# Attention and a gated feed-forward layer on one core: the gate's sigmoid computed as a tanh, single exps, and a new order of steps

## The chip, the core and the metric

The kernel runs on one core of one Trainium2 chip. The metric is the device time of one execution in microseconds (us); the number to be predicted is the median over several runs. The engines of the core have these names in the profile: PE is TensorE's matmul, PEld its weight load, DVE is VectorE, ACT is ScalarE, POOL is GpSimd, SP is SyncE, which here only issues DMAs.

## What is computed

Eight batches of 576 tokens. Attention is local: 8 heads of 64 channels, in blocks of 64 tokens. Its output x (4608 rows of 512 channels) goes through a feed-forward layer with a gate that is made by a short convolution along the tokens.

```python
scores = (1 / sqrt(64)) * q_c @ k_c.T          # blocks of 64 x 64
attn = exp(scores - max(scores)); attn = attn / (sum(attn) + 1e-9)
x = attn @ v_c                                  # heads side by side: 512 channels
h = maximum(x @ w_in, 0.0)                      # w_in 512 x 1024
conv_out[t] = sum over k of conv_w[k] * h[t + k - 1]
gate = 1.0 / (1.0 + exp(-conv_out))
out = (h * gate) @ w_out                        # w_out 1024 x 512
```

The three weight arrays come in 8-byte floats; q, k and v in 4-byte floats.

## The kernel before

**Precision.** Every operand of the two large products is split in a high and a low part (names ending in `_h` and `_l`), and a product is made as high times high, high times low and low times high.

**Attention.** The 4608 rows are 36 tiles of 128 (`att`, line 427). For the first 9 tiles q and k are loaded by rows (`load_rows`) and transposed on PE (`t_pe`, line 146) with an ACT copy behind it; for the others DVE transposes (`t_dve`, line 157). Then follow the scores on PE (line 173), `s_max` and `s_sub` on DVE (lines 183, 187), `s_exp` on ACT (line 192), `s_sum`, `s_eps`, `s_rec` on DVE (lines 196, 199, 202), `s_norm` on POOL (line 205), the transpose `p_pe` on PE (line 212) with `p_copy` on ACT, the product with v on PE (`attn_v`, line 225), and the split of the result by `x_hi` on ACT and `x_lo` on DVE (lines 249, 253).

**First product and gate.** The rows are also cut into 16 units of 288 tokens (`NU`, `HS`). For a unit and each of the 8 slices of 128 columns of `w_in`, `block` (line 477) issues 12 matmuls (`mm1`, line 262) into one of three PSUM buffers `h_ps`, `h_relu` and `c_mid` on ACT (lines 268, 273), `c_left` and `c_right` on DVE (lines 277, 283), `c_sig` on ACT (line 288), `c_mul` on DVE (line 291), which is the last reader of `h_ps` and frees it, `g_hi` on ACT (line 300) and `g_lo` on POOL (line 304).

**Second product.** For each of the 36 output tiles and each of the 8 slices, `mm2` (line 315) issues three matmuls into `o_ps`; after the eighth slice `o_copy` on ACT (line 320) moves the sum to SBUF and `o_store` on SP writes it out.

**Weights.** Ten slices of the two weight arrays (four of them half as wide) and the small conv_w are loaded and split in high and low by `split` (line 401): for one slice DVE does `w_mask`, `w_rest`, `w_low`, `w_sign`, `w_pow` (lines 344, 353, 357, 362, 370), ACT `w_bias`, `w_hi`, `w_lo_copy` (lines 349, 366, 381) and POOL `w_lo_big` (line 378). The raw bytes lie in one of two buffers until `w_sign` is done.

**The order.** The kernel collects all of this as steps (`step`, line 68), each with its engine, an assumed cost and a key. A planner (lines 584 to 677) goes through the steps with a model of engines and buffers: of the steps that can start within 0.6 us of the earliest on an engine it takes the one with the lowest key, with a penalty for a later start. The instructions are then issued in that order, and a chain of dependencies (lines 688 to 693) holds each engine to it. A key is the value written where the step is made, plus an offset by the kind of step (`by_step`), plus half an offset by chain (`by_chain`, line 566; a chain is the steps that share one `st`, in the order in which they were made). A step of ACT that needs another activation table costs the planner 1.28 us more (line 630). The `s_exp` steps of a unit wait for all `s_sub` steps of that unit, except in unit 0, so that they stand together:

```python
            if u == 0:
                group_ = []
            else:
                group_ = exps.setdefault(u, [])
```

Until the first `mm2`, the kernel puts transposes of a unit matrix into the gaps that the plan leaves on PE (line 685); they compute nothing that is used.

Of the kernel before, what the change touches and what calls it, by code (L numbers as in the profile page):

```python
# [23 lines left out]
AF = mybir.ActivationFunctionType  # L24
ALU = mybir.AluOpType
# [5 lines left out]
def attn_ffn(ctx: ExitStack, tc: tile.TileContext, q, k, v, w_in, conv_w, w_out, out):  # L31
    nc = tc.nc
# [9 lines left out]
    HS = S // 2  # L42
# [8 lines left out]
    scale = 1.0 / float(D) ** 0.5  # L51
# [13 lines left out]

    steps = []

    def step(eng, cost, key, fn, args=(), after=(), take=(), free=(), lag=0.0, table=None, port=False, bank=None):

        s = dict(eng=eng, cost=cost, key=key, fn=fn, args=args, after=[a for a in after if a], take=take, free=free,
                 lag=lag, table=table, port=port, bank=bank)
        steps.append(s)
        return s

# [208 lines left out]
            op0=ALU.mult, op1=ALU.add)  # L285

    def c_sig(st):
        nc.scalar.activation(out=st["c"], in_=st["c"], func=AF.Sigmoid)  # L288

    def c_mul(st):  # L290
        nc.vector.tensor_tensor(out=st["c"], in0=st["h"][:, st["i0"]:st["i0"] + HS], in1=st["c"], op=ALU.mult)  # L291

    def g_views(u, f):
        g0 = HS * u % GR
# [22 lines left out]

    def o_copy(st):
        st["os"] = work.tile([P, 2 * DM], F32, name="wt")[:, 0:DM]
        nc.scalar.copy(out=st["os"], in_=st["o"])  # L320

    def o_store(st, t):
        nc.sync.dma_start(out=out_rows[P * t:P * t + P, :], in_=st["os"])
# [100 lines left out]
            s8 = step("DVE", b, key + 0.04, w_lo, (st, lo), [s4, s7], free=["wv", "we"], port=True)  # L424
        return [s6, s8]

    def att(t, key, load_key, exps, writes):


        st = {}  # L430
        if t < NAT:
            r = "wslot" if t in W_ROWS else "slot"
            ld = step("SP", 1.25, load_key, load_rows, (st, t), take=[(r, st)], lag=3.3)
            tt = []
            for i in range(2):
                s = step("PE", 0.44, key - 3, t_pe, (st, i), [ld, before.get("t")], take=["h", "qk"[i] + "T"], free=[r] if i else [])
                before["t"] = s
                tt.append(step("ACT", 0.59, key - 3, t_copy, (st, i), [s], free=["h"]))
            slot_users.append(s)
        else:  # L440
            ld = group(t // TG)
            tt = [step("DVE", 0.7, key - 3, t_dve, (st, t, i), ld, take=["qk"[i] + "T"]) for i in range(2)]
            tt[1]["after"].append(tt[0])
            if t % TG == TG - 1:
                tt[1]["free"] = ["grp"]
        ldv = step("SP", 2.65, load_key + 0.05 if t < 5 else key - 8, load_v, (st, t), [before.get("v")], take=["v"], lag=1.66)
        tt[0]["after"] += [before["T"]] if t else []
        s = step("PE", 0.47, key, scores, (st,), tt + [before.get("s")], take=[("sx", st, "s")], free=["qT", "kT"], bank="sx")
        before.update(v=ldv, T=tt[1], s=s)
        s = step("DVE", 0.69, key, s_max, (st,), [s], take=["m"], bank="sx")  # L450
        s = step("DVE", 0.68, key, s_sub, (st,), [s], take=["e"], free=["m", ("sx", "s")], bank="sx")
        exps.append(s)
        s = step("ACT", 0.63, key + 8, s_exp, (st,), exps, table="exp")
        s["after"] = exps
        s = step("DVE", 0.68, key + 9, s_sum, (st,), [s], take=["z"])
        s = step("DVE", 0.17, key + 9, s_eps, (st,), [s], port=True)
        s = step("DVE", 0.2, key + 9, s_rec, (st,), [s])
        s = step("POOL", 1.05, key + 9, s_norm, (st,), [s], free=["z"], port=True)
        s = step("PE", 0.44, key + 12, p_pe, (st,), [s], take=["pt"], free=["e"])
        s = step("ACT", 0.59, key + 12, p_copy, (st,), [s], take=["pT"], free=["pt"])  # L460
        s = step("PE", 0.47, key + 14, attn_v, (st,), [s, ldv], take=[("sx", st, "x")], free=["pT", "v"], bank="sx")
        n = len(x_views(st, t, x_h)) - 1
        s = step("ACT", 0.58 + 0.15 * n, key + 14, x_hi, (st, t), [s] + writes, bank="sx")
        return step("DVE", 0.69 + 0.1 * n, key + 14, x_lo, (st, t), [s], free=[("sx", "x")], bank="sx")
# [12 lines left out]
    def block(key, u, f, after):  # L477
        st = {}
        s = step("PE", 1.6, key, mm1, (st, u, f), after, take=["h"])
        m = s  # L480
        s = step("ACT", 0.4, key + 2, h_relu, (st,), [s])
        s = step("ACT", 0.55, key + 2, c_mid, (st, u, f), [s, cw_done], take=["c"])
        s = step("DVE", 0.52, key + 2, c_left, (st, u, f), [s])
        s = step("DVE", 0.52, key + 2, c_right, (st, u, f), [s])
        s = step("ACT", 0.44, key + 2, c_sig, (st,), [s], table="sig")
        s = step("DVE", 0.45, key + 2, c_mul, (st,), [s], free=["h"])
        s = step("ACT", 0.44, key + 2.5, g_hi, (st, u, f), [s] + ring.get((u, f), []))
        s = step("POOL", 0.81, key + 2.5, g_lo, (st, u, f), [s], free=["c"], port=True)
        return m, s
# [10 lines left out]
    key_of = {}  # L500
# [5 lines left out]
    wi_done, wo_done, x_done, mm1_of, g_done, ring = {}, {}, {}, {}, {}, {}  # L506
# [15 lines left out]
    for n in range(FT // 2):  # L522
        wo(n, U[1] - 6 + 8.0 * n, 5.0 + 2 * n, lo_pool=LP[4 + n] == "1")

    exps = {}
    for u in range(NU + 1):

        for t in tiles_for[u] if u < NU else []:

            over = [v_ for v_ in range(NU) if any(HS * v_ - 2 < P * t + P and P * t < HS * v_ + HS + 2 for _ in (0,))]  # L530
            writes = [mm1_of[v_ - NX, f] for v_ in over if v_ >= NX for f in range(FT)]
            if u == 0:
                group_ = []
            else:
                group_ = exps.setdefault(u, [])
            x_done[t] = att(t, key_of[t], 0.1 + 0.5 * t if t < 5 else 4.5 + t, group_, writes)
        if u < NU:
            for f in range(FT):

# [5 lines left out]
        for i, t in enumerate(outs_in[u] if u <= NU - 1 else []):  # L545
            st = {}
            prev = None
            for f in range(FT):
                key = U[u + 1] + (U[u + 2] - U[u + 1]) * (i + f / FT) / len(outs_in[u]) + 0.3
                units = [v_ for v_ in range(NU) if HS * v_ < P * t + P and P * t < HS * v_ + HS]  # L550
                prev = step("PE", 0.7, key, mm2, (st, t, f), [prev] + wo_done[f] + [g_done[v_, f] for v_ in units],
                            take=["o"] if f == 0 else [])
                mm2_of[t, f] = prev
            s = step("ACT", 0.58, key + 1, o_copy, (st,), [prev], take=["wt"], free=["o"])
# [1 line left out]


    by_step = {
        "w_load": 7, "w_mask": -3.5, "w_bias": -4, "w_rest": -3, "w_low": -3.5, "w_pow": -13.5, "c_sum": -27.5, "c_pe":
        -4, "c_copy": -5.5, "w_hi": 14, "w_lo_big": -4.5, "w_lo_copy": 4, "load_rows": -0.5, "t_pe": -4, "t_copy": -7.5,  # L560
        "load_v": 6, "scores": -0.5, "s_max": 6, "s_sub": -7, "s_exp": -12.5, "s_sum": -4, "s_eps": -9, "s_rec": 4,
        "s_norm": -29.5, "p_pe": 4.5, "p_copy": 3.5, "attn_v": 3, "x_lo": 1, "mm1": -0.5, "h_relu": 1, "c_mid": 2,
        "c_left": 1.5, "c_right": 3.5, "c_sig": -4, "c_mul": 5.5, "g_hi": 2, "g_lo": 24, "o_copy": 1.5, "o_store": 9,
        "load_group": 15, "load_part": 1.5, "t_dve": 19
    }
    by_chain = [
# [9 lines left out]
    ]  # L576
    chains = {}
    for s in steps:
# [19 lines left out]
    free_at = dict.fromkeys(early, 0.0)  # L598
    free_at.update(SP=0.7, ACT=3.0)
    port, other, share = {"DVE": 0.0, "POOL": 0.0}, {"DVE": "POOL", "POOL": "DVE"}, {"DVE": 0.2, "POOL": 0.137}  # L600
    dma_free, table, kind, bank = 0.0, "exp", 0, {}
    left = [len(a) for a in befores]
    begin, end = [0.0] * n_, [0.0] * n_
    order_ = []
# [4 lines left out]
    while any(ready.values()):  # L609
        best = None  # L610
        for e, cand in ready.items():
            picks = []
            for i in cand:
                s = steps[i]
# [8 lines left out]
                else:  # L623
# [3 lines left out]
                    for o, until_ in bank.get(s["bank"], {}).items():  # L627
                        if o != e:
                            t = max(t, until_ + late[e])
                    if e == "ACT" and s["table"] not in (None, table):  # L630
                        t += 1.28
                    if e == "PE":
                        t += turn.get((kind, kinds.get(s["fn"], 0)), (0.0, 0.0))[0]
                        key -= 6.0 if kind == kinds.get(s["fn"], 0) == 1 else 0.0
# [6 lines left out]
        assert best, [(steps[i]["eng"], steps[i]["fn"].__name__, steps[i]["args"][1:]) for c in ready.values() for i in c]  # L641
        t, e, i = best
        s, cost = steps[i], steps[i]["cost"]
        if e == "ACT":
            table = s["table"] or table
        if e == "PE":
            cost += turn.get((kind, kinds.get(s["fn"], 0)), (0.0, 0.0))[1]
            kind = kinds.get(s["fn"], 0)
# [71 lines left out]
```

## Time and profile before

| | us |
|---|---|
| median of 3 runs (lowest to highest) | 526.4 (525.32 to 527.32) |
| the profiled execution, device time | 526.21 |
| its span in the trace | 524.4 |

The profile shows one execution. The span is the time between its first and its last recorded event; the device time of the same execution is 1.8 us longer. Matmuls are pipelined and their ends are modelled, so that the duration of one matmul row overlaps the next; where the text gives a price for a group of matmuls it is taken from the start of one group to the start of the next, as the chain of work that ended last gives it.

### The profile page before, as it was taken

To read this page: it belongs to the slowest core of one execution; us is meant where nothing else is said; L and a number is where in the kernel's file an instruction comes from. 1 tells how busy PE (TensorE), PEld (TensorE's weight loads), DVE (VectorE), ACT (ScalarE), POOL (GpSimd) and SP (SyncE) were. 2 spreads that over 40 slices of the span, in tenths; PEclk is the share of its full clock that TensorE was granted. 3 is DMA by queue.
4 is the path that set the end of the run, shared out by engine and by line. 5 is a ranking of instruction groups with operands and counts; after the bars stand their busy time and mean duration, and the time that the engine had idled before them with its cause. 6 is when DMAs were issued, how large, how long until landed. Compare 5 with 4: busy or idle time off the path is not lost.

```text
span 524.4 us, 13247 instructions
## 1 busy us (share of the span) xinstructions
PE 512.5 (98%) x5150; PEld 455.8 (87%) x5150; DVE 357.5 (68%) x732; ACT 363.7 (69%) x812; POOL 171.9 (33%) x237
## 2 busy tenths in 40 slices
PE   8889999999999999999999999999999999999997
PEld 8789886999888898989889898888989889989985
DVE  5889999657867478678677548675856876755320
ACT  4668889767775767687767657575686858686430
POOL 1424645442332333242412423232341414242220
PEclk9999999999999999999999999999999999999999
DMA  8899460353234534532355354233463121000101
GB/s 216 205 229 250 134 160 20 70 100 95 47 66 89 108 98 93 122 56 48 80 129 94 74 125 79 55 68 68 107 110 84 42 61 42 1 21 21 42 34 47
DMA packets 183170, 47.04 MB, mean 90 GB/s; under 512 B 175404, under 2 KB 175428, under 8 KB 183108
## 3 DMA queue, kind: packets, MB, share of 16 engines
q1 hardware_dynamic: 183108, 46.20, 39.8%
q8 instruction: 40, 0.66, 0.5%
q14 instruction: 22, 0.18, 0.1%
HBM read 36.72 MB, written 9.44 MB: 88 GB/s over the span
## 4 chain that ended last, share of the span: by engine, by line
PE 84%; DVE 8%; DMA 5%; ACT 1%; POOL 1%; issue 0%; SPq 0%; DVEq 0%; ACTq 0%
PE o_ps L315 37%; PE h_ps L262 37%; DMA qk<-in_moe_w_in 4%; PE sx_ps L225 3%; PE sx_ps L173 3%; PE pt_ps L212 3%; DVE wv L357 2%; DVE wt L344 1%; DMA qk<-in_moe_conv_w 1%; DVE wt L362 1%; DVE c L277 1%; DVE wv L353 1%; DVE c L283 1%; DVE c L291 1%; POOL wv L378 0%; PE h_ps L151 0%
## 5 line engine op out<-in xcount | busy, mean ns | idle before, releaser
L304 POOL TENSOR_TENSOR g_l<-c,g_h 128x288 fp32r<-128x288 f32 (+8 forms) x184 | 114.0, 635 | 231.1 <-ACT g_h L300 220.0
L315 PE MATMUL o_ps<-wo_h,g_h 128*128 128x512 f32 x288 | 118.1, 410 | 0.0
L315 PE MATMUL o_ps<-wo_l,g_h 128*128 128x512 f32 x288 | 113.4, 394 | 0.5 <-ACT wo_l L381 0.5
L315 PE MATMUL o_ps<-wo_h,g_l 128*128 128x512 f32 x288 | 113.5, 394 | 0.0
L277 DVE SCALAR_TENSOR_TENSOR c<-h_ps,cw,c 128x287 f32<-128x287 f32 (+1 forms) x128 | 65.4, 512 | 66.6 <-ACT c L273 66.1
L262 PE MATMUL h_ps<-x_h,wi_h 128*128 128x290 f32 x512 | 91.7, 301 | 1.8 <-DVE c L291 1.7
L262 PE MATMUL h_ps<-x_l,wi_h 128*128 128x290 f32 x512 | 90.1, 298 | 0.0
L262 PE MATMUL h_ps<-x_h,wi_l 128*128 128x290 f32 x512 | 89.8, 297 | 0.0
L262 PEld LDWEIGHTS h_ps<-x_h,wi_h 128*128 128x128 f32 x512 | 79.2, 189 | 10.6 <-DVE c L291 3.5
L268 ACT ACTIVATE h_ps<-h_ps 128x290 f32<-128x290 f32 x128 | 50.8, 397 | 37.3 <-PE h_ps L262 36.5
L300 ACT CAST g_h<-c 128x288 fp32r<-128x288 f32 (+8 forms) x184 | 59.6, 357 | 24.3 <-DVE c L291 16.6
L262 PEld LDWEIGHTS h_ps<-x_h,wi_l 128*128 128x128 f32 x512 | 76.3, 190 | 0.0
L262 PEld LDWEIGHTS h_ps<-x_l,wi_h 128*128 128x128 f32 x512 | 76.2, 189 | 0.0
L288 ACT ACTIVATE c<-c 128x288 f32<-128x288 f32 x128 | 55.7, 443 | 29.0 <-DVE c L283 28.1
L291 DVE TENSOR_TENSOR c<-h_ps,c 128x288 f32<-128x288 f32 x128 | 56.7, 450 | 27.4 <-ACT c L288 25.4
L273 ACT ACTIVATE c<-h_ps,cw 128x288 f32<-128x288 f32 x128 | 63.7, 499 | 7.2 <-POOL g_l L304 0.4
L283 DVE SCALAR_TENSOR_TENSOR c<-h_ps,cw,c 128x288 f32<-128x288 f32 (+1 forms) x128 | 65.6, 513 | 3.0
L315 PEld LDWEIGHTS o_ps<-wo_h,g_l 128*128 128x128 f32 x288 | 54.2, 188 | 12.4
L315 PEld LDWEIGHTS o_ps<-wo_h,g_h 128*128 128x128 f32 x288 | 54.3, 189 | 9.2 <-ACT wt L320 0.6
L315 PEld LDWEIGHTS o_ps<-wo_l,g_h 128*128 128x128 f32 x288 | 54.3, 188 | 8.0 <-ACT wo_l L381 0.8
L205 POOL TENSOR_TENSOR e<-e,z 128x512 f32<-128x512 f32 x36 | 38.1, 1072 | 64.8 <-DVE z L202 54.3
L320 ACT COPY wt<-o_ps 128x512 f32<-128x512 f32 x36 | 21.0, 585 | 24.5 <-PE o_ps L315 23.9
(50 smaller groups left out, 562.6 us busy)
## 6 DMA issues: line engine op xcount, KB each, us to landing
v<-in_v SPq DMA_DIRECT2D x144, 64.0 KB, 2.5
out<-wt SPq DMA_DIRECT2D x36, 256.0 KB, 2.1
qk<-in_q SPq DMA_DIRECT2D x96, 48.0 KB, 2.1
qk<-in_k SPq DMA_DIRECT2D x96, 48.0 KB, 2.2
qk<-in_moe_w_out SPq DMA_DIRECT2D x4, 1024.0 KB, 5.6
qk<-in_q SPq DMA_DIRECT2D x96, 24.0 KB, 1.9
qk<-in_k SPq DMA_DIRECT2D x96, 24.0 KB, 1.8
qk<-in_moe_w_in SPq DMA_DIRECT2D x4, 512.0 KB, 5.2
```

The costliest lines, as they stand in the source:

```text
L205: nc.gpsimd.tensor_tensor(out=st["e"], in0=st["e"], in1=st["z"].rearrange("p (h o) -> p h o", o=1).broadcast_to([P, H, C]), op=ALU.mult)
L262: nc.tensor.matmul(h_ps[:, 0:XU], lhsT=wt[:, f // 2, kt, P * (f % 2):P * (f % 2) + P], rhs=xt[:, u % NX, kt, :], start=n == 0, stop=n == 3 ...
L268: nc.scalar.activation(out=st["h"][:, 0:XU], in_=st["h"][:, 0:XU], func=AF.Relu)
L273: nc.scalar.mul(out=st["c"], in_=st["h"][:, i0:i0 + HS], mul=cw[:, FT + f:FT + f + 1])
L277: nc.vector.scalar_tensor_tensor(out=c[:, a:HS], in0=st["h"][:, i0 + a - 1:i0 + HS - 1], scalar=cw[:, f:f + 1], in1=c[:, a:HS], op0=ALU.mu ...
L283: nc.vector.scalar_tensor_tensor(out=c[:, 0:b], in0=st["h"][:, i0 + 1:i0 + 1 + b], scalar=cw[:, 2 * FT + f:2 * FT + f + 1], in1=c[:, 0:b], ...
L288: nc.scalar.activation(out=st["c"], in_=st["c"], func=AF.Sigmoid)
L291: nc.vector.tensor_tensor(out=st["c"], in0=st["h"][:, st["i0"]:st["i0"] + HS], in1=st["c"], op=ALU.mult)
L300: nc.scalar.copy(out=g_h[:, f, gs], in_=st["c"][:, cs])
L304: nc.gpsimd.tensor_tensor(out=g_l[:, f, gs], in0=st["c"][:, cs], in1=g_h[:, f, gs].bitcast(F32), op=ALU.subtract)
L315: nc.tensor.matmul(st["o"], lhsT=gt[:, f, o:o + P], rhs=wt[:, f, :], start=f == 0 and n == 0, stop=f == FT - 1 and n == 2)
L320: nc.scalar.copy(out=st["os"], in_=st["o"])
```

## The change

The sigmoid becomes a tanh of half the argument, `c_mul` becomes (1 + tanh) times h, and the factor 1/2 moves into `o_copy`. Each `s_exp` waits for its own `s_sub` alone. The planner loses its notion of activation tables, and takes 0.52 us for `c_mul` where it took 0.45. All offsets of the order are new. Of `by_chain` (221 numbers before, as many after) the first line is shown.

```diff
     def c_sig(st):
-        nc.scalar.activation(out=st["c"], in_=st["c"], func=AF.Sigmoid)
+
+        nc.scalar.activation(out=st["c"], in_=st["c"], func=AF.Tanh, scale=0.5)
 
     def c_mul(st):
-        nc.vector.tensor_tensor(out=st["c"], in0=st["h"][:, st["i0"]:st["i0"] + HS], in1=st["c"], op=ALU.mult)
+        nc.vector.scalar_tensor_tensor(
+            out=st["c"], in0=st["c"], scalar=1.0, in1=st["h"][:, st["i0"]:st["i0"] + HS], op0=ALU.add, op1=ALU.mult)
...
     def o_copy(st):
         st["os"] = work.tile([P, 2 * DM], F32, name="wt")[:, 0:DM]
-        nc.scalar.copy(out=st["os"], in_=st["o"])
+        nc.scalar.mul(out=st["os"], in_=st["o"], mul=0.5)
...
-        exps.append(s)
-        s = step("ACT", 0.63, key + 8, s_exp, (st,), exps, table="exp")
-        s["after"] = exps
+        s = step("ACT", 0.63, key + 8, s_exp, (st,), [s])
...
-        s = step("ACT", 0.44, key + 2, c_sig, (st,), [s], table="sig")
-        s = step("DVE", 0.45, key + 2, c_mul, (st,), [s], free=["h"])
+        s = step("ACT", 0.44, key + 2, c_sig, (st,), [s])
+        s = step("DVE", 0.52, key + 2, c_mul, (st,), [s], free=["h"])
...
     by_step = {
-        "w_load": 7, "w_mask": -3.5, "w_bias": -4, "w_rest": -3, "w_low": -3.5, "w_pow": -13.5, "c_sum": -27.5, "c_pe":
-        -4, "c_copy": -5.5, "w_hi": 14, "w_lo_big": -4.5, "w_lo_copy": 4, "load_rows": -0.5, "t_pe": -4, "t_copy": -7.5,
-        "load_v": 6, "scores": -0.5, "s_max": 6, "s_sub": -7, "s_exp": -12.5, "s_sum": -4, "s_eps": -9, "s_rec": 4,
-        "s_norm": -29.5, "p_pe": 4.5, "p_copy": 3.5, "attn_v": 3, "x_lo": 1, "mm1": -0.5, "h_relu": 1, "c_mid": 2,
-        "c_left": 1.5, "c_right": 3.5, "c_sig": -4, "c_mul": 5.5, "g_hi": 2, "g_lo": 24, "o_copy": 1.5, "o_store": 9,
-        "load_group": 15, "load_part": 1.5, "t_dve": 19
+        "w_load": 5, "w_mask": -5, "w_bias": -1.5, "w_rest": -2, "w_low": 1.5, "w_sign": 0.5, "w_pow": -2, "c_sum": -31,
+        "c_pe": 3, "c_copy": -5, "w_hi": -3.5, "w_lo_big": -3.5, "w_lo_copy": 2.5, "load_rows": 1, "t_pe": -8, "t_copy":
+        -7.5, "load_v": 7.5, "scores": -1, "s_max": 5.5, "s_sub": -9, "s_exp": -12.5, "s_sum": -4.5, "s_eps": -6,
+        "s_rec": 5.5, "s_norm": -23, "p_pe": 2.5, "p_copy": 1, "attn_v": 4, "x_hi": -3, "x_lo": 0.5, "mm1": -0.5,
+        "c_left": 3.5, "c_right": 3, "c_sig": 3.5, "c_mul": 5.5, "g_hi": 1.5, "g_lo": 36, "o_copy": -2.5, "o_store": 9,
+        "load_group": 10, "load_part": 2.5, "t_dve": 23
     }
     by_chain = [
-        -4, -51, -13, -46, -1, -24, -46, 4, 2, -2, 8, 9, -27, -24, -22, -1, 20, -9, 5, -4, 6, -9, -12, 38, 19, 3, 12,
...
+        8, -112, 1, -59, 11, 1, -56, 10, 23, 17, 25, 33, -10, -6, 0, 22, 6, 23, -6, -5, 23, -2, 15, 46, 6, 8, 17, 11, 7,
...
-                    if e == "ACT" and s["table"] not in (None, table):
-                        t += 1.28
```

## Rows read from the trace of the kernel before

**Rows 1.** The page: busy us of each engine (share of the span) xinstructions.

```profile
PE 512.5 (98%) x5150; PEld 455.8 (87%) x5150; DVE 357.5 (68%) x732; ACT 363.7 (69%) x812; POOL 171.9 (33%) x237
```

**Rows 2.** Three stretches: start:end length, busy us, granted clock, DMA share, GB/s.

```profile
0.00:38.40 38.40, 33.85 (x478) 31.09 (x479) 28.43 (x57) 22.20 (x38) 11.69 (x15) 1.00 0.88 217
38.40:90.00 51.60, 48.12 (x467) 42.77 (x466) 49.04 (x86) 46.13 (x88) 27.31 (x21) 1.00 0.59 145
90.00:520.70 430.70, 430.52 (x4210) 381.93 (x4209) 280.02 (x591) 294.82 (x687) 132.94 (x202) 1.00 0.34 71
```

**Rows 3.** Chain of work that ended last: start us, length us, engine, line, count.

```profile
99.10 1.09 PE sx_ps L173 x64
...
156.22 4.88 PE h_ps L262 x36
...
466.12 0.44 PE pt_ps L212 x4
...
481.25 8.26 PE o_ps L315 x36
```

**Rows 4.** PE's groups by line, 90 to 520.7 us: xcount | busy, mean ns | idle before.

```profile
L315 PE MATMUL o_ps<-wo_h,g_h 128*128 128x512 f32 x277 | 113.4, 409 | 0.0
...
L262 PE MATMUL h_ps<-x_h,wi_l 128*128 128x290 f32 x455 | 79.8, 297 | 0.0
...
L225 PE MATMUL sx_ps<-pT,v 64*64 64x64 f32 x960 | 19.4, 222 | 0.1
```

**Rows 5.** The same view from 38.4 to 90 us.

```profile
L262 PE MATMUL h_ps<-x_h,wi_h 128*128 128x290 f32 x60 | 11.3, 310 | 1.8 <-DVE c L291 1.7
...
L685 PE MATMUL o_ps<-ident 128*128 128x128 f32 x63 | 8.3, 274 | 0.0
L315 PE MATMUL o_ps<-wo_h,g_h 128*128 128x512 f32 x11 | 4.7, 430 | 0.0
```

**Rows 6.** Whom PE waited for, 38.4 to 90 us: us in total, times, longest.

```profile
PE h_ps L262 <- DVE c L291: 1.7, 3, 0.9
...
PE pt_ps L212 <- POOL e L205: 0.3, 1, 0.3
```

**Rows 7.** Table loads of ACT, whole run, by line: xcount | busy, mean ns | idle.

```profile
L288 ACT ACT_TABLE_LOAD x15 | 19.2, 1283 | 0.3
...
L192 ACT ACT_TABLE_LOAD x14 | 18.0, 1283 | 0.2
```

**Rows 8.** ACT in order of time: the table loads before 90 us.

```profile
44.70 1.28 ACT L288 ACT_TABLE_LOAD   x1
...
79.11 1.28 ACT L192 ACT_TABLE_LOAD   x1
...
86.22 1.28 ACT L288 ACT_TABLE_LOAD   x1
```

**Rows 9.** One stretch, with the columns of rows 2.

```profile
41.00:94.00 53.00, 49.45 (x501) 43.58 (x500) 51.44 (x91) 47.48 (x94) 29.10 (x21) 1.00 0.53 136
```

**Rows 10.** DVE's w_low: its 1024-wide form in the mean, and one.

```profile
L357 DVE SCALAR_TENSOR_TENSOR wv<-qk,wv 128x1024 f32<-128x1024 uint32 x6 | 8.7, 1458 | 0.0
...
42.77 1.22 DVE L357 SCALAR_TENSOR_TENSOR wv<-qk,wv 128x1024 f32<-128x1024 uint32 x1
```

**Rows 11.** DVE, by form: two-operand products and three-operand ones.

```profile
L291 DVE TENSOR_TENSOR c<-h_ps,c 128x288 f32<-128x288 f32 x128 | 56.7, 450 | 27.4 <-ACT c L288 25.4
...
L277 DVE SCALAR_TENSOR_TENSOR c<-h_ps,cw,c 128x288 f32<-128x288 f32 x64 | 32.9, 515 | 40.5 <-ACT c L273 40.3
...
L375 DVE SCALAR_TENSOR_TENSOR we<-wv,we 24x128 f32<-24x128 f32 x1 | 0.3, 280 | 0.0
...
L384 DVE TENSOR_TENSOR wt<-wt,we 24x128 f32<-24x128 f32 x1 | 0.3, 278 | 0.0
```

**Rows 12.** ACT, by form: a copy and a product with a constant.

```profile
L320 ACT COPY wt<-o_ps 128x512 f32<-128x512 f32 x36 | 21.0, 585 | 24.5 <-PE o_ps L315 23.9
...
L381 ACT ACTIVATE wi_l<-wv 128x512 fp32r<-128x512 f32 x4 | 2.5, 630 | 2.6 <-POOL wv L378 2.6
```

More of the change, by code (lines that the diff above doesn't have):

```diff
@@ L66, in attn_ffn, with step @@
     steps = []
-    def step(eng, cost, key, fn, args=(), after=(), take=(), free=(), lag=0.0, table=None, port=False, bank=None):
+    def step(eng, cost, key, fn, args=(), after=(), take=(), free=(), lag=0.0, port=False, bank=None):
         s = dict(eng=eng, cost=cost, key=key, fn=fn, args=args, after=[a for a in after if a], take=take, free=free,
-                 lag=lag, table=table, port=port, bank=bank)
+                 lag=lag, port=port, bank=bank)
         steps.append(s)
@@ L425, in split, with att @@
         return [s6, s8]
-    def att(t, key, load_key, exps, writes):
+    def att(t, key, load_key, writes):
         st = {}
@@ L523, in attn_ffn @@
         wo(n, U[1] - 6 + 8.0 * n, 5.0 + 2 * n, lo_pool=LP[4 + n] == "1")
-    exps = {}
     for u in range(NU + 1):
@@ L531, in attn_ffn @@
             writes = [mm1_of[v_ - NX, f] for v_ in over if v_ >= NX for f in range(FT)]
[L532 to L536, printed above, removed]
+            x_done[t] = att(t, key_of[t], 0.1 + 0.5 * t if t < 5 else 4.5 + t, writes)
         if u < NU:
@@ L600, in attn_ffn @@
     port, other, share = {"DVE": 0.0, "POOL": 0.0}, {"DVE": "POOL", "POOL": "DVE"}, {"DVE": 0.2, "POOL": 0.137}
-    dma_free, table, kind, bank = 0.0, "exp", 0, {}
+    dma_free, kind, bank = 0.0, 0, {}
     left = [len(a) for a in befores]
@@ L643, in attn_ffn @@
         s, cost = steps[i], steps[i]["cost"]
-        if e == "ACT":
-            table = s["table"] or table
         if e == "PE":
```

16 rows, old and new, of the table by_chain are left out of this document.

## The prediction

> **What bounds the kernel.** I began with the page's busy times [rows 1]: PE stands at 98% of the span, ACT at 69%, DVE at 68%. That PE is busy does not say that it does useful work: until the first `mm2` it also runs transposes that fill gaps. So the second view was the windows, cut where the trace changes: at 38.4 us, where the first `mm1` starts, and at 90 us, behind the last wait of PE for another engine that is more than a change from one kind of matmul to the next [rows 2]. The granted clock is 1.00 in all three, so every price of PE below is one of the 2.4 GHz level.
>
> Third, the chain of work that ended last, for prices from start to start [rows 3]: 36 matmuls of `mm1` take 4.88 us, so a group of 12 costs 1.627; 36 of `mm2` take 8.26, so three cost 0.688; two tiles of scores (or of `attn_v`) take 1.09, one 0.545; one `p_pe` 0.44. With the counts behind 90 us [rows 4], `mm1` is 455 x 3 / 12 = 113.75 groups, 185.1 us; `mm2` 277 groups, 190.6 us; attention 960 / 32 = 30 tiles at 2 x 0.545 + 0.44 = 1.53, 45.9 us. Together 421.6 of 430.7 us. What is left, 9.1 us or 2%, is the price of changing between kinds of matmul. **From 90 us on the kernel is PE's bare work**; nothing that ACT, DVE or POOL save there can show in the time, except as fewer changes of kind.
>
> Between 38.4 and 90 us it is otherwise. Useful are 15 groups of `mm1` (24.4 us), 11 of `mm2` (7.6) and a few tiles of attention; fillers take 8.3 us and PE waits 1.7 us for `c_mul` and 0.3 for `s_norm` [rows 5, 6]. What binds PE there is DVE: from 41 to 94 us it is busy 51.44 of 53.0 us, ACT 47.48 [rows 9]. DVE splits the weights and does the convolution of the first blocks at once. Ahead of 38.4 us DVE is busy 28.43 us and the DMA engines 88% [rows 2]: it is the loads that rule.
>
> **The change part by part.** The sum is made against the profiled execution, 526.21 us (span 524.4 and 1.8 around it); the median is 526.4, 0.2 above it.
>
> *Table loads.* 15 + 14 = 29 loads of 1.283 us go, 37.2 us of ACT [rows 7]. Behind 90 us lie 26 of them, 33.4 us, hidden by PE's own work; if that cover were gone (PE waiting for ACT), up to 33.4 us would show. Ahead of 90 us are three: at 44.70 and 86.22, each in front of a `c_sig`, whose `c_mul` frees the `h_ps` that an `mm1` wants, and at 79.11 in front of two exps [rows 8]. They cost at most 3 x 1.283 = 3.8 us, and nothing if DVE, full as it is, takes up what ACT gives. The nearest rows are PE's own waits for what hangs on these loads, 1.7 + 0.3 = 2.0 us [rows 6]; I take **-2.0**, ends 0 and -3.8.
>
> Between a load and the activation behind it the trace shows next to no idle time, 0.3 us over 15 loads [rows 7]. The Trainium skill ("ScalarE: Activation LUTs", section "What ACT_TABLE_LOAD costs") puts a drain of 1380 ns beside the load and 2.66 us on a switch; by that page three switches would be 8.0 us and this term, scaled alike, -4.2, for a time of 519.8. The trace does not agree, so the sum keeps 1.283.
>
> *tanh for sigmoid* is the same kind of activation on the same 128x288 tile; the scale of 0.5 is a constant of the instruction. I take 0; ACT has 51.6 - 46.13 = 5.5 us free in the middle stretch [rows 2], so that a few per cent on 15 of them would be covered.
>
> *`c_mul`* gets a third operand, a constant. With a constant such an instruction took 280 ns where a product of two took 278, at 24x128; `c_left`, whose scalar is a column of a tile, takes 515 where `c_mul` takes 450 [rows 11]. So a call costs 2 to 65 ns more; 15 calls lie ahead of the point where PE is full, 0.03 to 1.0 us. A gain is excluded, since the tiles stay and an operation is added. The constant is the nearer row: **+0.1**. The other 113 calls are up to 7.3 us of DVE, hidden since DVE is busy 280 of 430.7 us behind 90 [rows 2].
>
> *`o_copy`* as a product: a copy of 128x512 takes 585 ns, a product with a constant from SBUF 630 [rows 12]. All but the last are beside PE's work; the last is on the path, 0 to +0.05. I take 0.
>
> *Exps that no longer wait* for each other can start some us sooner in each unit. Behind 90 us PE stands 0.1 us for `attn_v` [rows 4] and has `mm1` and `mm2` queued, so nothing is gained; in a unit without such cover it would be one wait of `p_pe`, 0.3 us where it shows now [rows 6]. Counted in the term above.
>
> *The new order* moves every step on every queue. For SP I worked the keys of the loads out of the offsets: before and after, the first are one half slice of w_in, one full slice, then the rows of tiles 0 to 2, then two half slices (which change places), conv_w, the last half slice, the fourth slice; w_out follows. So the loads that rule the first 38.4 us come in nearly the same order, and I leave that stretch as it is. POOL has 51.6 - 27.31 = 24 us free in the middle stretch, and the DMA engines are at 59% there [rows 2]; so what is moved past their queues (`s_norm`, `g_lo`, `w_lo_big`, loads and stores) has room. A gain is bounded by all that PE now loses: 8.3 + 1.7 + 0.3 = 10.3 us in the middle, the 38.4 - 28.43 = 10.0 us in which DVE stands idle ahead of it, and 9.1 us of changes of kind, 29.4 together. The end below is in the rivals, +6.1. What a new order can do in the stretch that DVE binds is nearer to two rows: DVE's idle time there, 53.0 - 51.44 = 1.56 us [rows 9], and the passes that other engines stretch, such as `w_low`, 1458 ns in the mean where one alone took 1220, six times 0.24 = 1.4 us [rows 10]. That is 3.0 us; I take **-2.5**.
>
> *Sum:* -2.0 + 0 + 0.1 + 0 - 2.5 = -4.4; 526.21 - 4.4 = 521.8, and 0.2 for the median: **522.0 us**. What is late next is again PE's bare work behind 90 us.
>
> **The rivals.** (A) *The order closes most of the gaps in the middle.* If 10.3 us of fillers and waits shrink to a third (-6.9), and the changes of kind by a fifth (-1.8), the time is 526.4 - 8.7 = 517.7, and up to 12 us less than before where the first `mm1` also comes sooner. For: these losses exist and are PE's. Against: DVE is full in that stretch.
>
> (B) *Nothing shows.* DVE binds from 41 to 94 us and no DVE pass is removed; ACT's 3.8 us are then hidden like the other 33.4, and the time stays at 526.4, give or take 2. For: rows 9. This holds too the case that the change does not do what it says: if tanh were still served by a table other than that of exp, 29 loads would remain and the sum without its first term gives 524.0. The Trainium skill ("ScalarE: Activation LUTs", "Table sets: the hidden batching unit") lists tanh in the set of exp and also in that of sigmoid; the trace of before holds no tanh and cannot say which one is taken. I give that 4 in 100, inside B.
>
> (C) *Slower: `c_mul` late behind weight passes.* There are three `h_ps`, and each is freed by `c_mul` alone. DVE works in the planned order; a `c_mul` placed behind one more 1.22 us pass [rows 10] holds an `h_ps`, and the next `mm1` waits. The planner no longer prices a table and prices `c_mul` at 0.52, so where it puts it among the passes is new. In five wide slices that is 5 x 1.22 = 6.1 us, with the dear `c_mul` 1.0 more: 526.4 + 7.1 = 533.5. It decides from the point where PE's wait for `c_mul` in that stretch grows from 1.7 us to some 6. For: a full DVE. Against: the longest such wait now is 0.9 us, and the loads gone give ACT's side of that loop 1.28 us back each time.
>
> **How the numbers follow.** A measurement of this kernel tells about 0.5%, 2.6 us, from no change. My forecast with its near surroundings (519 to 523.8) has 0.42, A 0.20, B 0.25, C 0.13. Faster by over 0.5% is the forecast and A, 0.62; within it B, 0.25; slower C, 0.13. The range reaches from 515.5, leaving the best fourth of A or so, to 528.5, which takes in B with c_mul's upper price and the mildest of C; outside are some 0.05 below and 0.12 above.
>
> **What would show it.** In the changed profile: one table load in all, at the start; ACT busy some 37 us less; the `c_mul` line at 450 to 515 ns, near the lower; PE packed as before behind some 90 us, with PE's rows there unchanged in count and price; the first `mm1` again near 38 us; fewer fillers than 63 behind it, and PE's wait for `c_mul` under 1.7 us. The forecast is wrong if the first `mm1` moves by more than 2 us, if the fillers grow, if PE waits for another engine behind 90 us, or if the gain stands behind 90 us in fewer changes of kind.

## The result and the profile after

The changed kernel takes 521.72 us (median of 5 runs, 520.14 to 522.55) against 526.4 for the kernel before: ratio 0.9914, 95% interval 0.9886 to 0.9941, some 4.5 us or 0.9% less. The forecast was 522.0. The profiled execution of the changed kernel took 520.14 us (span 518.0) and is the fastest of its five, that of before, 526.21, is near its median; so of the 6.1 us between the two profiles about 1.4 is scatter, a source of which is shown in the last section.

The page, busy time of each engine, to be read beside [rows 1]:

```profile
PE 508.4 (98%) x5128; PEld 452.9 (87%) x5128; DVE 354.6 (68%) x732; ACT 327.0 (63%) x783; POOL 172.5 (33%) x237
```

ACT is busy 36.7 us less and issues 29 instructions fewer. All the table loads are gone but the one at the start, line by line:

```profile
L292 DVE SCALAR_TENSOR_TENSOR c<-c,h_ps 128x288 f32<-128x288 f32 x128 | 57.2, 448 | 24.2 <-ACT c L289 22.6
...
L322 ACT ACTIVATE wt<-o_ps 128x512 f32<-128x512 f32 x36 | 21.4, 598 | 20.1 <-PE o_ps L317 19.6
...
L81 ACT ACT_TABLE_LOAD x1 | 1.3, 1283 | 0.7 <-PEq L695 0.7
```

`c_mul` with its third operand takes 448 ns where it took 450, the output copy 598 where it took 585 [rows 11, 12]. None of this is yet time. For that, the three stretches of [rows 2]; the last `mm2` now ends at 514.2 us:

```profile
0.00:38.40 38.40, 34.55 (x483) 31.45 (x484) 28.70 (x58) 23.36 (x41) 11.75 (x15) 1.00 0.92 215
38.40:90.00 51.60, 49.69 (x562) 44.70 (x561) 50.42 (x90) 45.51 (x95) 29.02 (x22) 1.00 0.57 148
90.00:514.20 424.20, 424.16 (x4088) 376.72 (x4086) 275.53 (x586) 257.52 (x648) 131.74 (x200) 1.00 0.34 72
```

Behind 90 us PE works for 424.2 us where it worked for 430.7, and is as full as before. Its groups there say why it is done sooner:

```profile
L317 PE MATMUL o_ps<-wo_h,g_h 128*128 128x512 f32 x276 | 113.3, 410 | 0.0
...
L262 PE MATMUL h_ps<-x_l,wi_h 128*128 128x290 f32 x452 | 79.6, 298 | 0.0
...
L225 PE MATMUL sx_ps<-pT,v 64*64 64x64 f32 x928 | 18.7, 222 | 0.0
L173 PE MATMUL sx_ps<-kT,qT 64*64 64x64 f32 x864 | 17.6, 221 | 0.0
L212 PE MATMUL pt_ps<-ident,e 128*128 128x128 f32 x116 | 17.5, 273 | 0.0
```

The groups are fewer than in [rows 4], at the same prices. At the prices of [rows 3], `mm1` is 452 + 448 + 452 matmuls or 112.7 groups (183.3 us), `mm2` 276 (189.9), attention 29 + 27 groups of 32 at 0.545 and 29 of `p_pe` at 0.44 (43.3): 416.5 of 424.2 us. Counted in the same way, the kernel before has 421.6 of 430.7: 113.25 groups of `mm1` (184.3), 277 of `mm2` (190.6), and in attention 30 + 29 groups of 32, 29 of `p_pe` and 4 of `t_pe`, taken at the price of `p_pe` (46.7). So **5.1 us of useful work have moved ahead of 90 us, and 1.4 us less are lost in changes of kind** (PE changes kind 254 times there instead of 269). What PE does from 38.4 to 90 us, beside [rows 5]:

```profile
L262 PE MATMUL h_ps<-x_l,wi_h 128*128 128x290 f32 x62 | 11.0, 298 | 0.0
L675 PE MATMUL o_ps<-ident 128*128 128x128 f32 x39 | 5.2, 275 | 0.0
L151 PE MATMUL h_ps<-ident,qk 128*128 128x128 f32 x32 | 5.1, 283 | 1.2 <-DVE c L292 1.2
L317 PE MATMUL o_ps<-wo_h,g_h 128*128 128x512 f32 x12 | 5.0, 418 | 0.0
...
L225 PE MATMUL sx_ps<-pT,v 64*64 64x64 f32 x128 | 2.8, 224 | 0.3 <-ACT pT L217 0.3
L173 PE MATMUL sx_ps<-kT,qT 64*64 64x64 f32 x128 | 2.7, 221 | 0.0
```

39 fillers instead of 63, and in their place attention of later tiles: 8 groups of `t_pe` (32 matmuls by four) where there were 4, 4 groups of scores instead of 2, 4 of `attn_v` instead of 3. That is 4 x 0.44 + 3 x 0.545 = 3.4 us; `mm1` has a third of a group more and `mm2` one group, 1.2 us. PE's waits in the stretch are 1.9 us, where they were 3.3. The first `mm1` starts at 37.64 us.

### The profile page after: what moved, and what is told of

The parts are those of the page before. It is cut to its first block, busy times and chain, and to the rows that moved or that the text cites. A ratio compares the mean times of both kernels' runs of the same rounds, so it can differ in the third digit from the quotient of the medians.

```text
span 518.0 us, 13170 instructions
## 1 busy us (share of the span) xinstructions
PE 508.4 (98%) x5128; PEld 452.9 (87%) x5128; DVE 354.6 (68%) x732; ACT 327.0 (63%) x783; POOL 172.5 (33%) x237
## 4 chain that ended last, share of the span: by engine, by line
PE 85%; DVE 8%; SPq 2%; DMA 2%; ACT 1%; issue 1%; POOL 0%; DVEq 0%; ACTq 0%
PE o_ps L317 39%; PE h_ps L262 36%; PE sx_ps L225 4%; PE sx_ps L173 3%; PE pt_ps L212 3%; SPq L111 1%; DVE wv L359 1%; DMA v<-in_v 1%; DMA qk<-in_moe_w_in 1%; DVE c L277 1%; SPq L143 1%; DVE c L283 1%; DVE wv L355 1%; DVE wt L346 1%; DVE wt L364 1%
## 5 line engine op out<-in xcount | busy, mean ns | idle before, releaser
L262 PEld LDWEIGHTS h_ps<-x_h,wi_l 128*128 128x128 f32 x512 | 76.4, 190 | 0.0
L292 DVE SCALAR_TENSOR_TENSOR c<-c,h_ps 128x288 f32<-128x288 f32 x128 | 57.2, 448 | 24.2 <-ACT c L289 22.6
L253 DVE TENSOR_TENSOR x_l<-sx_ps,x_h 128x512 fp32r<-128x512 f32 (+2 forms) x56 | 25.8, 497 | 17.9 <-ACT x_h L249 16.8
```

What stands on the lines that cost most here:

```text
L253: nc.vector.tensor_tensor(out=lo, in0=src, in1=hi.bitcast(F32), op=ALU.subtract)
L262: nc.tensor.matmul(h_ps[:, 0:XU], lhsT=wt[:, f // 2, kt, P * (f % 2):P * (f % 2) + P], rhs=xt[:, u % NX, kt, :], start=n == 0, stop=n == 3 ...
L292: nc.vector.scalar_tensor_tensor(out=st["c"], in0=st["c"], scalar=1.0, in1=st["h"][:, st["i0"]:st["i0"] + HS], op0=ALU.add, op1=ALU.mult)
```

## Experiments

Each ratio is against runs of the kernel before on the same chip, with its 95% interval. Differences to the 521.7 us of the changed kernel compare runs that were not made side by side; taken from the ratios, the costs below are 0.5 to 0.8 us larger, and the gain without `w_low` is 0.3 smaller.

**The tanh gate in the old order**, to the letter: `c_sig`, `c_mul` and `o_copy` of the change in the kernel before, the planner untouched.

```diff
-        nc.scalar.activation(out=st["c"], in_=st["c"], func=AF.Sigmoid)
+        nc.scalar.activation(out=st["c"], in_=st["c"], func=AF.Tanh, scale=0.5)
...
```

> The old order of steps to the letter (the planner's offsets, costs and table rule of before), with the tanh gate, its product and the halved output copy alone. Theory (table loads ahead of 90 us cost 2 us, the new order is worth the rest): one table load in the trace, 524.4 us, ACT busy 37 us less, PE's wait for c_mul between 38 and 90 us below 1.7 us, the fillers still 229. Rival 1 (the order alone makes the gain, the loads are all hidden): 526.4 us. Rival 2 (the loads alone make it, wherever they lie): 521.7 us.

525.77 us, ratio 1.0002 (0.9993 to 1.0011). **All 29 loads are gone, and nothing is gained.** The reason can be read in DVE's queue. These are DVE's instructions up to the `c_mul` that stood behind the first load [rows 8], in order of time, in the kernel before (start us, length us):

```profile
43.90 0.51 DVE L283 SCALAR_TENSOR_TENSOR c<-h_ps,cw,c 128x288 f32<-128x288 f32 x1
44.33 1.22 DVE L362 SCALAR_TENSOR_TENSOR wt<-qk,wt 128x1024 uint32<-128x1024 uint32 x1
45.65 0.69 DVE L370 TENSOR_SCALAR we<-wt 128x1024 uint32<-128x1024 uint32 x1
46.26 0.51 DVE L277 SCALAR_TENSOR_TENSOR c<-h_ps,cw,c 128x287 f32<-128x287 f32 x1
46.69 0.45 DVE L291 TENSOR_TENSOR c<-h_ps,c 128x288 f32<-128x288 f32 x1
```

and with tanh in the same order:

```profile
42.21 0.51 DVE L283 SCALAR_TENSOR_TENSOR c<-h_ps,cw,c 128x288 f32<-128x288 f32 x1
42.64 1.22 DVE L363 SCALAR_TENSOR_TENSOR wt<-qk,wt 128x1024 uint32<-128x1024 uint32 x1
43.96 0.69 DVE L371 TENSOR_SCALAR we<-wt 128x1024 uint32<-128x1024 uint32 x1
44.57 0.51 DVE L277 SCALAR_TENSOR_TENSOR c<-h_ps,cw,c 128x287 f32<-128x287 f32 x1
45.00 0.44 DVE L291 SCALAR_TENSOR_TENSOR c<-c,h_ps 128x288 f32<-128x288 f32 x1
```

From `c_right` to `c_mul` it is 2.79 us in both. DVE has two weight passes and a convolution pass to do in between, and the load lay beside them. In front of the 14 `c_mul` from 38.4 to 90 us DVE stood idle 0.2 us in all, in the kernel before:

```profile
L291 DVE TENSOR_TENSOR c<-h_ps,c 128x288 f32<-128x288 f32 x14 | 6.1, 448 | 0.2 <-ACT c L288 0.2
```

**Loads back in the early units only**: as the last, but units 0 and 1 keep the sigmoid. Three loads then stand ahead of 90 us and one behind, at 113.6.

```diff
+        if st["u"] < 2:
+            nc.scalar.activation(out=st["c"], in_=st["c"], func=AF.Sigmoid)
+        else:
+            nc.scalar.activation(out=st["c"], in_=st["c"], func=AF.Tanh, scale=0.5)
...
```

> As the run with the old order and tanh, but units 0 and 1 keep the sigmoid (their product is then the gate times two, so that the halved output copy fits), so that the loads ahead of 90 us stay and those behind go. Theory (only loads ahead of 90 us count): 526.4 us, no change against the kernel before. Rival 2 (loads count wherever they lie): some 26/29 of the gain of the run with tanh everywhere.

525.5 us, ratio 1.0002 (0.9990 to 1.0014). Together with the run before it: neither the loads ahead of 90 us nor those behind cost the old order anything that can be measured.

**The sigmoid in the new order**, to the letter, with the old `c_mul` and `o_copy`.

```diff
-        nc.scalar.activation(out=st["c"], in_=st["c"], func=AF.Tanh, scale=0.5)
+        nc.scalar.activation(out=st["c"], in_=st["c"], func=AF.Sigmoid)
...
```

> The new order to the letter, with sigmoid, the product of two and the plain output copy, so that the table loads come back, now around each exp that stands alone: some 55 loads, 70 us of ACT, about 9 of them ahead of 90 us. Theory: behind 90 us PE's own work hides most of them, ahead of 90 us ACT has 6 us free and the loads stand before c_mul: some 5 us over the changed kernel, 526 to 528 us. Rival 1 (loads hidden everywhere): 521.7 us. Rival 2: as many loads more than the kernel before as should make it slower than before, 530 us or more, with PE waiting behind 90 us too.

552.29 us, ratio 1.0510 (1.0486 to 1.0534), more than any of the theories gave but the last. By line, and then whom PE waits for over the whole run:

```profile
L289 ACT ACT_TABLE_LOAD x28 | 35.9, 1283 | 0.5
L192 ACT ACT_TABLE_LOAD x27 | 34.6, 1283 | 0.5
```

```profile
PE h_ps L262 <- DVE c L292: 15.2, 11, 2.5
PE pt_ps L212 <- ACT pT L217: 3.6, 2, 2.3
PE pt_ps L212 <- POOL e L205: 2.3, 4, 1.2
```

55 loads, 70.6 us of ACT, cost 31 us, also behind 100 us. This order can only be had with one table. Three more runs put a price on the loads there: **sigmoid in units 0 and 1 alone**, **from unit 2 on alone**, and **in the fifth slice of units 0 and 1 alone**, each as the diff above with its own condition.

> The changed kernel, order untouched, with the sigmoid in units 0 and 1 alone (their product is the gate times two, so that the halved output copy fits): table loads come back ahead of some 100 us only, about 9 of them, 11 to 12 us of ACT where it has 6 us free. Theory as it now stands (in the new order ACT's time ahead of 90 us is spent on attention brought forward, and the loads would take it away): 527 to 531 us, the loss between 38 and 100 us. Rival 1 (loads are hidden in any order): 521.7 us.

531.55 us, ratio 1.0116 (1.0097 to 1.0134), just above the range.

> The complement: sigmoid in units 2 to 15, tanh in units 0 and 1, order untouched, some 46 table loads, 59 us of ACT, behind 100 us. If PE's own work hides loads there as it hid 26 of them in the old order: 521.7 us. If each pair of loads around a lone exp holds up what PE wants next, PE waits for c_mul behind 100 us: 540 to 546 us, the rest of the 552.3 that sigmoid everywhere took.

543.71 us, ratio 1.0343 (1.0324 to 1.0362). Behind 90 us PE's work, at the prices of [rows 3], is the same 416.5 us as in the changed kernel; the rest of that stretch, changes of kind and waits, is 31.7 us instead of 7.7.

> The changed kernel, order untouched, with the sigmoid in one block of unit 0 and one of unit 1 alone (the fifth slice of each), so that four table loads, 5.1 us of ACT, stand ahead of 90 us. Theory as it now stands (ACT has about 6 us free there, but a load stands in front of a c_mul that frees a buffer): 523 to 526 us. If loads ahead of 90 us cost nothing, as in the old order: 521.7 us. If each costs its full length: 526.8 us.

524.06 us, ratio 0.9967 (0.9950 to 0.9985). Against 521.7 us, the early loads (12 in the trace, 8 of them ahead of 100 us) cost 9.8 us, the 47 late ones 22.0, together the 30.6 of sigmoid everywhere within 1.3. The four loads of the last run cost 2.3 us, 0.6 each, which is little more than the intervals leave open; two of them stand ahead of 90 us (47.82 and 49.96), not four as expected, and two behind (94.63 and 102.53). In the old order the four loads of units 0 and 1 were free. Behind 90 us the prediction's words "hidden by PE's own work" held for 26 loads in the old order and not for 47 around lone exps.

**Old offsets with the new steps, and new offsets with the old steps.**

```diff
     by_step = {
-        "w_load": 5, "w_mask": -5, "w_bias": -1.5, "w_rest": -2, "w_low": 1.5, "w_sign": 0.5, "w_pow": -2, "c_sum": -31,
...
+        "w_load": 7, "w_mask": -3.5, "w_bias": -4, "w_rest": -3, "w_low": -3.5, "w_pow": -13.5, "c_sum": -27.5, "c_pe":
...
```

`by_chain` goes back in the same way.

> The changed kernel with the old offsets by kind of step and by chain: tanh, single exps, the planner without tables and with the dearer c_mul, but the offsets that belonged to the old steps. Theory (the order was fitted to its steps and the fit is worth some 2.5 us): 524 us, between the two kernels. Rival 1 (the structure brings it by itself, offsets nothing): 521.7 us. Rival 3 (an order that is not fitted loses more than the structure gains): over 526.4 us.

532.79 us, ratio 1.0138 (1.0125 to 1.0151).

> The kernel before (sigmoid, exps of a unit together, planner with tables) with the new offsets. If an order is good only with the steps it was fitted to, as the old offsets were with the new steps at 532.8 us: 528 to 540 us. If the new offsets are better by themselves: 521 to 525 us.

533.55 us, ratio 1.0148 (1.0125 to 1.0171). **All offsets by chain at zero**, in the changed kernel:

> The changed kernel with all 221 offsets by chain at zero, those by kind of step kept. If the gain lies in an order that is fitted to its steps, most of it goes: 526 to 535 us, with the loss ahead of 100 us and, less, in changes of kind on PE behind it. If the offsets by kind carry it: 521 to 523 us.

528.80 us, ratio 1.0047 (1.0029 to 1.0064). Three orders that are not fitted to their steps are all slower than before: with none of these offsets does the structure give a gain by itself, and with the new steps the old offsets are worse than none by chain. In the run with old offsets PE runs 87 fillers from 38.4 to 90 us, and in that without offsets by chain 85, where the changed kernel has 39. Fillers are not the whole loss: the run with new offsets and old steps has 60, fewer than the kernel before. Behind 90 us the useful work of the three runs, 421 to 423 us, is what it was before, but the rest of that stretch is 14.0 us with the old offsets, 10.6 with none by chain and 15.8 with new offsets and old steps, against 9.1 before and 7.7 in the changed kernel.

**Less and more work on DVE**, order untouched: the changed kernel without `w_low` (the low parts of the weights then lack their low bits), and with `w_rest` done twice.

```diff
-        nc.vector.scalar_tensor_tensor(out=st["V"], in0=st["L"], scalar=2.0 ** -32, in1=st["V"].bitcast(U32), op0=ALU.mult, op1=ALU.add)
+        pass
```

> The changed kernel, order untouched, without w_low (the low bits of the weights are left out of the low parts), which takes 11.4 us off DVE, nearly all of it ahead of 94 us. Theory (from 41 to 94 us DVE binds, and PE makes good what DVE is spared there): 514 to 518 us, with the first mm1 about where it was and fewer waits and fillers' worth of lost time behind it. Rival 4 (the loads or ACT bind that stretch): within 2 us of 521.7.

518.37 us, ratio 0.9855 (0.9841 to 0.9870), just short of the range.

> The changed kernel, order untouched, with w_rest done twice for each slice, some 7 us more on DVE ahead of 94 us and nothing else. Theory (DVE binds there): 525 to 528 us, with PE waiting for c_mul several us more. Rival 4: within 2 us of 521.7.

525.72 us, ratio 1.0000 (0.9990 to 1.0010). `w_low` took 11.4 us, of which 5.9 lie behind 41 us, and leaving it out gained 3.4. The two passes of `w_rest` together took 9.4 us more than the one did, of which the added pass has 4.3 between 41 and 94 us, and cost 4.0. Ahead of 41 us the relief changed nothing (first `mm1` at 37.65 us, against 37.64); with the added pass the first `mm1` came at 38.97, so a part of the 4.0 arose there, or is scatter. From 41 to 94 us, in the changed kernel, without `w_low`, and with `w_rest` twice:

```profile
41.00:94.00 53.00, 51.09 (x570) 45.95 (x570) 51.69 (x96) 46.36 (x96) 31.42 (x23) 1.00 0.54 141
```

```profile
41.00:94.00 53.00, 52.70 (x582) 47.87 (x581) 48.17 (x96) 48.50 (x102) 33.28 (x26) 1.00 0.57 147
```

```profile
41.00:94.00 53.00, 48.39 (x541) 42.28 (x543) 51.95 (x92) 44.22 (x91) 28.51 (x22) 1.00 0.53 140
```

DVE binds the stretch, as [rows 9] had it: relieved, it has 4.8 us free and PE is fuller; burdened, it stays full and PE empties. PE makes good a good half of what DVE is spared inside the stretch, not all of it. Its queue is fixed: without `w_low` PE is busy 52.70 of 53.0 us, and the 39 fillers, 5.2 us, still stand where the plan put them.

**One load moved in the kernel before.** SP's queue differs ahead of 41 us in a way that the prediction had missed: the old order issues the rows of tile 6 ahead of the fourth slice of w_in, the new one behind it. (Loads of v have moved among the rows and half slices too; they were not tried by themselves.)

```diff
+    wide_ = [i for i in range(n_) if steps[i]["fn"] is w_load][6]
+    rows_ = next(i for i in range(n_) if steps[i]["fn"] is load_rows and steps[i]["args"][1] == 6)
+    begin[rows_] = begin[wide_] + 0.01
```

> The kernel before, sigmoid and all, with one load moved: the fourth slice of w_in is issued ahead of the rows of tile 6 instead of behind them, as the new order has it; every other instruction keeps its place. In the traces the slice landed 10.2 us after its issue before and 7.3 us after the change, and DVE began on it at 41.1 and 37.7 us. If the earlier landing is what the new order gains ahead of 45 us and DVE's queue passes it on: 523 to 524.5 us, DVE beginning on the slice 2 to 3 us sooner. If DVE only waits for something else then, or the late rows of tile 6 cost as much: 525.8 us, and the gain lies in what DVE and PE do in which order.

525.78 us, ratio 1.0013 (1.0003 to 1.0023), a hair slower. The slice landed 7.1 us after its issue, as in the new order, and DVE began on it at 39.91 us, 1.2 us sooner than before. (One execution's start does not show the move by itself: with tanh in the old order and no load moved, DVE began at 39.45.) What took the 1.2 us back stands six microseconds later, on ACT and then on DVE:

```profile
44.65 1.28 ACT L288 ACT_TABLE_LOAD   x1
45.94 0.45 ACT L288 ACTIVATE c<-c 128x288 f32<-128x288 f32 x1
```

```profile
46.42 0.46 DVE L291 TENSOR_TENSOR c<-h_ps,c 128x288 f32<-128x288 f32 x1 [0.52 <-ACT c L288]
...
49.76 0.68 DVE L344 TENSOR_SCALAR wt<-qk 128x1024 uint32<-128x1024 uint32 x1
```

With DVE ahead of its old time, the table load that had cost nothing is what DVE waits for, 0.52 us, besides shorter waits for `c_mid` and the next `c_sig`; at the next slice, 49.76 us, it is where it was in the kernel before. The earlier slice and the missing load each give nothing alone. Whether the two together, without the rest of the new order, would gain was not tried.

## Why the prediction was right, point by point

*What bounds the kernel.* Right. PE's bare work behind 90 us is unchanged in price, the first `mm1` is near 38 us, DVE is the bound from 41 to 94 us, and most of what was gained was gained by work that PE did ahead of 90 us. Two of the signs given for this did not quite hold: PE's rows behind 90 us are fewer, since work has moved, and 1.4 of the 6.5 us saved there are changes of kind.

*Table loads, -2.0 us.* The term that failed: in the old order it measured 0 (-0.4 to +0.6 us by the interval). The end at 0 was the true one. The step took PE's waits for `c_mul` and `s_norm` as what hangs on the loads; but a wait for `c_mul` is not a wait for the table load in front of `c_sig` when DVE, in the order of its queue, could not have come to `c_mul` any sooner. The row that would have told it is DVE's own idle time in front of `c_mul` ahead of 90 us, of which there was next to none.

*The new order, -2.5 us.* Right in sign and place, half the size: the new order with tanh against the old order with tanh is 0.9914 to 1.0002, 4.6 us. The step took it from what DVE could do sooner, 3.0 us. It missed that the order can also change what PE does while it waits for DVE: attention takes the place of fillers, which also needs ACT for its copies. The profile of the run with tanh in the old order, like this one the fastest of its runs, has a span of 522.6 us, 4.6 more. The same count behind 90 us gives it 419.9 us of work in 428.8, so of the 4.6 us 3.4 are work moved ahead of 90 us and 1.2 fewer changes of kind. From 38.4 to 90 us it has 20 fillers more than the changed kernel, and 3.1 us of waits of PE instead of 1.9:

```profile
L686 PE MATMUL o_ps<-ident 128*128 128x128 f32 x59 | 7.7, 274 | 0.0
```

The sum of PE's losses in that stretch also left out two waits, which [rows 6] do not show and which are gone in the changed kernel; with them PE waited 3.3 us before, not 2.0:

```profile
PE sx_ps L173 <- DVE e L187: 0.8, 1, 0.8
PE o_ps L315 <- ACT wo_l L381: 0.5, 1, 0.5
```

ACT's work from 38.4 to 90 us without loads was 46.13 - 3 x 1.283 = 42.3 us (43.6 with tanh in the old order) and is now 45.5. So the loads' time went, it seems, not to PE directly but to ACT work brought forward. That this order needs ACT's time is shown by the loads put back; whether the old steps, tuned afresh, could gain as much with their loads was not tried. The two errors, +2.0 and -2.1, cancel: that the sum came out within 0.3 us of the measured median is luck.

*`c_mul`, +0.1, and `o_copy`, 0.* 448 against 450 ns and 598 against 585: right in size, by the nearer row with a constant; that a gain is excluded was not right, since `c_mul` takes 2 ns less. *Exps that no longer wait*: no run has them alone; with the sigmoid their order brings 55 loads, so here they rest on the tanh.

*SP's queue.* The keys gave the loads "in nearly the same order"; in the trace a weight slice and the rows of a tile are exchanged against the keys, perhaps since a weight slice also waits for its buffer, and loads of v have moved. The exchange alone was worth nothing. *Table load against the page.* The Trainium skill's 2.66 us for a switch ("ScalarE: Activation LUTs", "What ACT_TABLE_LOAD costs") found no support: before 55 loads ACT stood 1.0 us idle in all, and in the kernel before what follows a load begins within 0.02 us of its end. The Trainium skill's list that puts tanh in the set of exp ("ScalarE: Activation LUTs", "Table sets: the hidden batching unit") agrees with the trace, one load in all.

*The rivals.* (A), gaps closed by 8.7 us: its mechanism, in part. (B), nothing shows: true of the tanh alone. (C), `c_mul` late behind weight passes: PE's waits that name `c_mul` from 38.4 to 90 us are 1.6 us (0.4 at `mm1`, 1.2 at `t_pe`, which uses the `h_ps` buffers too and which (C) left out), no longer than before; but with an order that is not fitted the kernel is 2 to 8 us slower than before, so a loss of that size was near.

## What to carry to other kernels

An instruction taken off an engine that is not the bound gives time only if the order then uses it: here 37 us of ACT gave nothing in the old order, and came with 4.6 us in a new one that needs it. Before a wait is priced by the instruction that released it, look whether the releasing engine's own queue would have come there sooner. When an order written by a planner is tuned, tune it again after each change of a step; the old tuning can be worse than before the change.

## What was not expected of the hardware

Executions of one order differ by when the first loads land, and the span follows to within 0.9 us. DVE's first pass over the fourth slice in three kernels with the same order, the kernel before, with tanh in the old order, and with tanh from unit 2 on:

```profile
41.13 0.69 DVE L344 TENSOR_SCALAR wt<-qk 128x1024 uint32<-128x1024 uint32 x1 [0.60 <-DMA qk<-in_moe_w_in]
```

```profile
39.45 0.69 DVE L345 TENSOR_SCALAR wt<-qk 128x1024 uint32<-128x1024 uint32 x1
```

```profile
42.34 0.69 DVE L351 TENSOR_SCALAR wt<-qk 128x1024 uint32<-128x1024 uint32 x1 [1.24 <-DMA qk<-in_moe_w_in]
```

The spans are 524.4, 522.6 and 526.4 us; less these starts 483.3, 483.2 and 484.1. The twelve runs of the last kernel alone lie between 524.81 and 528.24 us. So two profiles can differ by 3 us with no cause in the program, and a change of 1% has to be judged from medians.

A long wait of PE can be paid twice. In the run with the sigmoid in units 0 and 1, PE in order of time around its longest wait:

```profile
51.02 0.60 PE L212 MATMUL pt_ps<-ident,e 128*128 128x128 f32 x4
53.97 1.33 PE L262 MATMUL h_ps<-x_h,wi_h 128*128 128x290 f32 x4 [2.34 <-DVE c L297]
55.10 1.17 PE L262 MATMUL h_ps<-x_l,wi_h 128*128 128x290 f32 x4
56.06 1.17 PE L262 MATMUL h_ps<-x_h,wi_l 128*128 128x290 f32 x4
57.16 0.69 PE L225 MATMUL sx_ps<-pT,v 64*64 64x64 f32 x32
```

After 2.34 us without work the group of 12 takes 57.16 - 53.97 = 3.2 us where it takes 1.6; the granted clock of the two 4 us stretches there is 0.72 and 0.86, that is 4 x 0.28 + 4 x 0.14 = 1.7 us of full speed lost, and in single microseconds it is 0.50, the 1.2 GHz level, from 54 to 57 us. A second such wait, of 1.93 us up to 76.4 us, costs as much. So up to 3.4 of the 9.8 us of that run are lost by way of the clock; sigmoid everywhere has three such places in its first 150 us, up to 5 of its 31 us. But the length of a wait does not decide it. Waits of 1.2 us, the longest in the changed kernel behind the first matmul, show no fall; with new offsets and old steps the clock fell to 0.50 from 84 to 87 us behind waits of 1.17 and 0.68 us. And with sigmoid everywhere, waits of 1.90, 2.04 and 2.34 us, up to 76.9, 88.0 and 217.6 us, show none. The second of them, and the stretch behind it, where the granted clock stays at 1.00:

```profile
88.02 0.66 PE L151 MATMUL h_ps<-ident,qk 128*128 128x128 f32 x4 [2.04 <-DVE c L292]
```

```profile
88.00:92.00 4.00, 3.65 (x53) 3.11 (x54) 3.87 (x7) 3.91 (x8) 2.80 (x2) 1.00 0.09 20
```

What decides whether the clock falls these runs do not show.
